# More spin matmuls in the first chunk, fillers and masks moved in units 5 and 6, and the last rows split 256 to 128

## The chip, the cores and the metric

The kernel runs on one core of a Trainium2 chip. The metric is device time in microseconds (us) of one execution; lower is better. Before the change, seven runs gave a median of 205.24 us, from 203.64 to 206.64. All times of single instructions come from one profiled execution.

The engines are called PE (matrix multiplication; its weight loads are listed as PEld), DVE (vector), ACT (activation and copies), POOL (the general engine GpSimd) and SP (which issues most transfers). Each works through its own queue in order, and they wait for one another through semaphores. PE writes to PSUM, from which DVE and ACT read.

## The reference

A recurrent attention layer with a decaying state, and after it a two-layer network. Batch 4, 8 heads, 768 steps, head width 48; the network goes from 384 to 2048 and back to 384, all in float32.

```python
def _attn_ref(r, k, v, w, u):
    for t in range(S):
        cur = np.einsum('bhd,bhe->bhde', u[None] * kt, vt)
        y[:, :, t] = np.einsum('bhd,bhde->bhe', rt, state + cur)
        state = w[None, :, :, None] * state + np.einsum('bhd,bhe->bhde', kt, vt)
    return y

def _moe_ref(x, w_in, w_out):
    h = x @ w_in
    g = h * (1.0 / (1.0 + np.exp(-h)))
    return g @ w_out
```

The output of the first, with the heads side by side (3072 x 384), is the input x of the second.

## The kernel before

The steps of time are cut into 6 chunks of 128, and a unit is one chunk of one batch: 24 units, numbered chunk by chunk, so that units 0 to 3 are the first chunk, 4 to 7 the second (B is 4 in the code). Inside a chunk the recurrence is written as a masked product, and the state is carried from chunk to chunk. The tiles run on a schedule written by hand: the order of the calls in the program is the order in each engine's queue.

For one unit the steps are these.

- `load` (lines 64 to 73): SP loads r, k and v, 192 KB each, into one of six sets of buffers.
- `nat_v`, `nat_ku`, `nat_rk`, `nat_kc` (172 to 192): ACT makes v in 16 bits; POOL makes ku = k times u, rku_f = r times ku, and kc, k scaled for the state.
- `p1` (214), or its two halves `p1t` (232) and `p1d` (249): PE transposes r and k into PSUM (tiles tr and tk, later xs), and DVE multiplies them by powers of the decay (tile rk).
- `bonus_sum` (194) and `bonus_vu` (200): DVE sums rku_f to rku, one number for each head, and POOL makes vu = v times rku. For unit 0, ACT makes vu (`bonus_act`, 207).
- `p2` (261): PE makes the score matrices ae and ao of the even and odd heads, and DVE masks them (tile am). With `nxt` given it also holds the transposes of the next unit, and their products unless `late` is set.
- `p3y` (283) and `p3e` (297): PE makes y from the masked scores and v, and from the second chunk on from the state; DVE adds vu and writes y in 16 bits (y16).
- `sums` (302) and `state` (312): PE makes the unit's share of the state (sps), DVE adds it to the state, and POOL decays it (sdec).
- `p4` (334): PE transposes y16 (yT), and ACT copies that into xT, the input of the network.

The network's work is a list of fillers. `l1` (348) makes 128 of the 2048 middle columns of one chunk: three matmuls on PE (tile hps) with w_in, and the activation on ACT (tile gT). `l2` (361) makes a quarter of the sum for 128 output rows (tile ops), four matmuls with w_out, and after the last quarter DVE copies the rows and SP stores them. `fill(n)` (397) takes fillers from the list up to a weight of n; a whole `l1` or an `l2` quarter weighs 1, an `l1` of two batches 0.5 (three matmuls of 256 columns). What a `fill` could not take is carried to the next one, up to a weight of 1.

The last 128 rows of output are made by `l2_last` (374), in two halves of 192 columns, each with 16 matmuls, a copy on DVE and a store.

w_in comes in four slices (`win_part`, 412) and w_out in two halves (`wout_part`, 416), issued by POOL in line with its other work: the first half of w_out at line 524, the second at line 530, after the `nat_kc` of unit 5.

`spin` (118) issues matmuls of 128 x 128 by 512 zeros, whose result nobody reads. Without a tile given it takes one from the five PSUM slots with the tag "t", which the transposes, scores, y, sps and yT share. Spins stand at the start (lines 137 and 139), before the transposes of unit 1 and before the scores of unit 1.

The order around the changed places is: `p2(1)`, rku and vu of unit 1, `p3e(0)`, `p3y(1)`, `p3e(1)`, `p4(0)`, `p1(2)`, the loads of the next chunk, `p4(1)`, and then the first fillers (lines 445 to 464). In the second chunk: `p2` of unit 5, fillers, `p3y`, `p3e`, `p1d` of unit 6, sums, fillers, `p4` of unit 5, fillers, a new list of fillers (542 to 554). From unit 6 on a loop (566 to 596) runs over the units.

Of the kernel before, what the change touches and what calls it, by code (L numbers as in the profile page):

```python
# [8 lines left out]
FP = mybir.dt.float32  # L9
# [6 lines left out]
def kernel(  # L16
# [11 lines left out]
    nc = tc.nc  # L28

    B, H, S, D = r.shape  # L30
    C = 128
    NCH = S // C
    HD = H * D
# [6 lines left out]
    NU = B * NCH  # L40
# [5 lines left out]
    wrk = ctx.enter_context(tc.tile_pool(name="wrk", bufs=2))  # L46
# [12 lines left out]
    wout = big.tile([128, NFT, HD], F16)  # L59

    def unit(i):
        return divmod(i, B)
# [29 lines left out]
    for t in (rin, kin):  # L92
# [7 lines left out]
        out=maskM, in_=maskM, compare_op=ALU.is_ge, fill=0.0,  # L100
# [17 lines left out]
    def spin(n, t=None):  # L118

        if t is None:  # L120
            t = ps.tile([128, 512], FP, name="spin", tag="t", bufs=5)
        else:
            t = t.rearrange("s p t -> s (p t)")
        for _ in range(n):
            nc.tensor.matmul(t, junk[:, 0:128], junk, start=True, stop=True)  # L125

    def to_cols(row, copy):
        t = ps.tile([128, 512], FP, name="cols", tag="t", bufs=5)
        nc.tensor.transpose(t[0:PR, 0:NP], row.rearrange("p j d -> p (j d)")[:, 0:PR],
                            ident[0:NP, 0:NP])  # L130
        if copy is None:
            return t[0:PR, 0:NP]
        c = cst.tile([PR, NP], FP, name="cols_sb")
        copy(out=c, in_=t[0:PR, 0:NP])
        return c

    spin(5)
    wT = to_cols(wrow, None)
    spin(5)
    u_bc = cst.tile([128, H, D], FP)  # L140
    lamC = cst.tile([128, H, D], FP)

# [12 lines left out]
    while n < C:  # L155
        nc.vector.tensor_tensor(
            out=pi[:, :, 1 + n:1 + 2 * n], in0=pi[:, :, 1:1 + n],
# [31 lines left out]
    def nat_kc(i):  # L189
        n = i % NIN  # L190
        nc.gpsimd.tensor_tensor(out=kc[i % NKC][:, :, 0:D], in0=kin[n][:, :, 0:D],  # L191
                                in1=lamC, op=ALU.mult)

    def bonus_sum(i):
        L = live[i]
        L["rku"] = wrk.tile([128, H], FP, name="rku", bufs=3)
        nc.vector.tensor_reduce(out=L["rku"], in_=L["rku_f"], axis=mybir.AxisListType.X,  # L197
                                op=ALU.add)
# [33 lines left out]
    def p1t(i):  # L232

        n = i % NIN
        L = live.setdefault(i, {})
        xs = [ps.tile([128, 2, NP, 64], FP, name="xs", tag="t", bufs=5) for _ in range(2)]
        for a, src in enumerate((rin, kin)):
            flat = src[n].rearrange("p h d -> p (h d)")
            for p in range(NP):
                for g in range(2):  # L240
                    t = slice(64 * g, 64 * g + 64)
                    nc.tensor.transpose(xs[g][0:PR, a, p, :],  # L242
                                        flat[t, 128 * p:128 * p + PR], ident[t, t])
        rk = wrk.tile([PR, 2, NP, C], FP, name="rk")
        L["rT"] = rk[:, 0]
        L["kT"] = rk[:, 1]
        L["xs"] = xs, rk

    def p1d(i):
        L = live[i]  # L250
        xs, rk = L["xs"]
        for g in range(2):
            nc.vector.tensor_tensor(out=rk[:, :, :, 64 * g:64 * g + 64], in0=xs[g][0:PR],  # L253
                                    in1=lam(g), op=ALU.mult)

    def r16(i):
        L = live[i]
        L["rT16"] = wrk.tile([PR, NP, C], F16, name="rT16")
        nc.scalar.copy(out=L["rT16"], in_=L["rT"])

    def p2(i, spins=0, nxt=None, late=False):
        L = live[i]
        ae = ps.tile([128, NP, C], FP, name="ae", tag="t", bufs=5)
        ao = ps.tile([128, NP, C], FP, name="ao", tag="t", bufs=5)
        spin(spins, ae)
        for p in range(NP):
            nc.tensor.matmul(ae[:, p, :], L["kT"][0:D, p, :], L["rT"][0:D, p, :],  # L267
                             start=True, stop=True)
            nc.tensor.matmul(ao[:, p, :], L["kT"][64:PR, p, :], L["rT"][64:PR, p, :],  # L269
                             start=True, stop=True)  # L270
        if nxt is not None:
            p1t(nxt)
        L["am"] = []
        for a in (ae, ao):
            am = wrk.tile([128, NP, C], F16, name="am", bufs=4)
            nc.vector.tensor_tensor(out=am, in0=a,  # L276
                                    in1=maskM.unsqueeze(1).broadcast_to([128, NP, C]),
                                    op=ALU.mult)
            L["am"].append(am)
        if nxt is not None and not late:  # L280
            p1d(nxt)

    def p3y(i):
        sc, b = unit(i)
        L = live[i]
        v16 = L["v16"]
        L["y"] = y = ps.tile([128, H, D], FP, name="y", tag="t", bufs=5)
        for p in range(NP):
            if sc:
                nc.tensor.matmul(y[:, 2 * p:2 * p + 2, :], L["rT16"][:, p, :],  # L290
                                 st16[b][:, p, :], start=True, stop=False)
            for j in range(2):
                nc.tensor.matmul(y[:, 2 * p + j, :], L["am"][j][:, p, :],  # L293
                                 v16[:, 2 * p + j, :], start=not sc,
                                 stop=(not sc or j == 1))

    def p3e(i):
        L = live[i]
        L["y16"] = wrk.tile([128, H, D], F16, name="y16")
        nc.vector.tensor_tensor(out=L["y16"], in0=L["y"], in1=L["vu"], op=ALU.add)  # L300
# [33 lines left out]
    def p4(i):  # L334
        sc, b = unit(i)
        L = live[i]
        if sc not in xts:
            xts[sc] = wrk.tile([128, NQ, B, C], F16, name="xT", bufs=3)
        yT = ps.tile([128, NQ, C], F16, name="yT", tag="t", bufs=5)
        yf = L["y16"].rearrange("p h d -> p (h d)")  # L340
        for q in range(NQ):
            nc.tensor.transpose(yT[:, q, :], yf[:, 128 * q:128 * q + 128], ident16)  # L342
        nc.scalar.copy(out=xts[sc][:, :, b, :], in_=yT)  # L343


    gts = {}
# [27 lines left out]
    def l2_last(sc, b):  # L374

        tt = b * S + sc * C
        for n0 in (0, HD // 2):
            ops = ps.tile([128, HD], FP, name="ops", tag="moe", bufs=3)
            for ft in range(NFT):
                nc.tensor.matmul(ops[:, 0:HD // 2], gts[sc][:, ft, b * C:(b + 1) * C],  # L380
                                 wout[:, ft, n0:n0 + HD // 2],
                                 start=(ft == 0), stop=(ft == NFT - 1))
            osb = wrk.tile([128, HD // 2], FP, name="osh")
            nc.vector.tensor_copy(out=osb, in_=ops[:, 0:HD // 2])
            nc.sync.dma_start(out=out[tt:tt + C, n0:n0 + HD // 2], in_=osb)

    def l1s(sc, b0=0, b1=B):
        return [((b1 - b0) / B, lambda ft=ft: l1(sc, ft, b0, b1)) for ft in range(NFT)]

    def l2s(sc, b0=0, b1=B):  # L390
        return [(1.0, lambda b=b, part=part: l2(sc, b, part))
                for b in range(b0, b1) for part in range(4)]
# [4 lines left out]
    def fill(n):  # L397
        owed[0] = min(owed[0] + n, n + 1.0)
        while fillers and owed[0] > 0.01:
            w_, f = fillers.pop(0)  # L400
            owed[0] -= w_
            f()
# [44 lines left out]
    bonus_vu(1)  # L447
    p3e(0)
    nat_kc(0)
    p3y(1)  # L450
    p3e(1)
    p4(0)
    p1(2)
    nat_ku(2)
# [5 lines left out]
    load(B + 1)  # L460
    p4(1)
    nc.scalar.copy(out=st[2], in_=zero)
    fillers.extend(l1s(0, 0, 2))
    fill(.5)
    nat_v(2)
# [31 lines left out]
    def front(i):  # L497
        nat_v(i)
        nat_ku(i)
        nat_rk(i)  # L500
        nat_kc(i)
# [38 lines left out]
        load(NIN + i)  # L540
    fill(.5)
    p2(b_, nxt=b_ + 1, late=True)
    fill(1)
    p3y(b_)
    p3e(b_)
    p1d(b_ + 1)
# [3 lines left out]
    load(NIN + 5)  # L550
    fill(.5)
    p4(b_)
    fill(1.5)
    fillers.extend(l1s(1, 0, 2) + l2s(0))
    sums(b_)
    state(b_)
# [8 lines left out]
    half_state(1)  # L565
    for i in range(B + 2, NU):
        sc, b = unit(i)
        bonus_sum(i)
        bonus_vu(i)
        p2(i, nxt=i + 1 if i + 1 < NU else None)  # L570
        fill(2)
        if i + 1 < NU:
            front(i + 1)
        if i >= NIN:
            load(i + NIN)
        fill(1)
        p3y(i)
        p3e(i)
        if sc < NCH - 1:
            sums(i)  # L580
            state(i)
        fill(2)
        p4(i)
        if i + 1 < NU:
            r16(i + 1)
        if i == B + 2:
            half_state(3)
        fill(1)
        if sc == 1:
            half_state(b)  # L590
        fill(2)
        if b == B - 1:
            if sc == 1:
                fillers.extend(l1s(1, 2, 4) + l2s(1))
            else:
                fillers.extend(l1s(sc) + l2s(sc))
# [32 lines left out]
```

## Time and profile before

| what | value |
|---|---|
| median of 7 runs | 205.24 us (203.64 to 206.64) |
| profiled execution: its own time | 204.11 us |
| profiled execution: span | 202.4 us |
| mean granted clock of PE | 0.992 |
| busy: PE, DVE, POOL, ACT | 192.5, 115.2, 115.0, 97.8 us |
| PE on ops (L366), hps (L354), scores (L267, in the chain) | 65.5 us, 70.3 us, 11% of the span |
| PE waiting for masks before y (L293) | 2.5 us |
| loads of r, k, v, issue to landing (median) | 3.5 to 3.8 us |
| w_out halves, issue to landing | 9.7 and 11.6 us |

The time of the execution is longer than the span by 1.7 us, what lies around the profiled program. A row of the page's table of groups reads: line, engine, operation, output from input, how many, then busy us and mean ns of one, then the idle time ahead of them and what ended it. The row of forty slices gives tenths of busy time; PEclk in it is the granted clock of PE in tenths. In the rows by stretches, each engine has its busy time and, in brackets, the number of its instructions. The chain of waits goes back from the last instruction, at each step to what released it; its rows give the start, the length, the engine, the tile and the line.

### The profile page before, as it was taken

The numbers are of one execution on the slowest core, as the hardware profiler recorded it, in microseconds if no ns is written. First come the engines' busy times: TensorE is split into PE (matmuls) and PEld (weight loads), VectorE is DVE, ScalarE is ACT, GpSimd is POOL, SyncE is SP. The second block draws the span as 40 slices with busy tenths as digits, with TensorE's granted clock in tenths as the row PEclk, the third lists the DMA queues.
The fourth block names the chain that finished last, engine by engine and source line by source line (L and its number), as shares of the span: only waits on it lengthen the run. The fifth ranks groups of instructions, "written<-read, shape, count | busy, mean of one in ns | idle before, by whom it ended". The sixth has DMA issues, their size and how long they took to land.

```text
span 202.4 us, 5004 instructions
## 1 busy us (share of the span) xinstructions
PE 192.5 (95%) x1967; PEld 130.7 (65%) x1967; DVE 115.2 (57%) x233; ACT 97.8 (48%) x225; POOL 115.0 (57%) x145
## 2 busy tenths in 40 slices
PE   7868999998999999999999999999999999999993
PEld 2647878786667777675666765666765666744563
DVE  6785658858559548595546865546864635510121
ACT  2564677797430680218772029772029661069300
POOL 3579967979954854957774757571738370100000
PEclk9996999999999999999999999999999999999999
DMA  4999999999999920759631639201120001110022
GB/s 85 201 191 154 175 223 181 180 186 200 175 226 219 225 49 28 169 125 219 129 63 56 144 95 190 45 0 42 39 79 3 0 3 40 70 50 0 0 78 78
DMA packets 82207, 22.34 MB, mean 110 GB/s; under 512 B 75400, under 2 KB 82184, under 8 KB 82184
## 3 DMA queue, kind: packets, MB, share of 16 engines
q1 hardware_dynamic: 78504, 18.88, 43.5%
q0 software_dynamic: 3680, 3.15, 10.4%
q8 instruction: 15, 0.25, 0.5%
q14 instruction: 8, 0.07, 0.1%
HBM read 20.45 MB, written 4.72 MB: 124 GB/s over the span
## 4 chain that ended last, share of the span: by engine, by line
PE 87%; DVE 6%; issue 2%; ACT 2%; POOL 1%; DVEq 0%; POOLq 0%
PE ops L366 30%; PE hps L354 27%; PE ae L267 11%; PE xs L242 4%; DVE am L276 3%; PE y L293 3%; PE yT L342 2%; PE spin L125 2%; PE y L290 2%; PE sps L309 1%; PE ops L380 1%; DVE y L300 1%; PE tk L223 1%; PE tr L223 1%; ACT xT L343 1%
## 5 line engine op out<-in xcount | busy, mean ns | idle before, releaser
L357 ACT ACTIVATE gT<-hps 128x256 f16<-128x256 f32 (+1 forms) x128 | 59.6, 493 | 25.6 <-PE hps L354 23.8
L354 PE MATMUL hps<-xT,win 128*128 128x256 f16 (+1 forms) x384 | 70.3, 327 | 1.0 <-ACT xT L343 0.6
L366 PE MATMUL ops<-wout,gT 128*128 128x384 f16 x368 | 65.5, 326 | 0.0
L354 PEld LDWEIGHTS <-win 128*128 128x128 f16 x384 | 35.2, 98 | 22.6 <-issue 1.6
L366 PEld LDWEIGHTS <-gT 128*128 128x128 f16 x368 | 34.2, 98 | 21.1
L343 ACT COPY xT<-yT 128x384 f16<-128x384 f16 x24 | 11.4, 476 | 58.8 <-PE yT L342 58.8
L276 DVE TENSOR_TENSOR am<-ae,maskM 128x512 f16<-128x512 f32 x24 | 16.6, 691 | 37.1 <-PE ao L269 36.9
L203 POOL TENSOR_TENSOR vu<-vin,rku 128x384 f32<-128x384 f32 x23 | 19.1, 829 | 21.1 <-DVE rku L197 21.0
L370 DVE COPY osb<-ops 128x384 f32<-128x384 f32 x23 | 12.8, 555 | 29.2 <-PE ops L366 29.0
L267 PEld LDWEIGHTS ae<-rk 48*128 48x128 f32 x192 | 23.2, 187 | 7.8 <-issue 5.7
L267 PE MATMUL ae<-rk 48*128 48x128 f32 x192 | 27.8, 285 | 0.4 <-DVE rk L230 0.4
L269 PE MATMUL ao<-rk 48*128 48x128 f32 x192 | 27.8, 285 | 0.0
L253 DVE TENSOR_TENSOR rk<-xs,pif 112x512 f32<-112x512 f32 x40 | 25.5, 680 | 1.7 <-PE xs L242 1.7
L186 POOL TENSOR_TENSOR rku_f<-rin,ku 128x384 f32<-128x384 f32 x24 | 24.1, 1005 | 1.9
L180 POOL TENSOR_TENSOR ku<-kin,u_bc 128x384 f32<-128x384 f32 x24 | 24.1, 1002 | 1.4 <-DMA kin<-in_k_dram 1.4
L191 POOL TENSOR_TENSOR kc<-kin,lamC 128x384 f16<-128x384 f32 x24 | 24.0, 1003 | 0.0
L269 PEld LDWEIGHTS ao<-rk 48*128 48x128 f32 x192 | 23.2, 187 | 0.0
L323 POOL CAST stb<-st 112x384 f16<-112x384 f32 x12 | 6.0, 502 | 25.8 <-DVE st L318 25.8
L300 DVE TENSOR_TENSOR y<-y,vu 128x384 f16<-128x384 f32 x24 | 13.3, 553 | 7.8 <-PE y L293 7.2
L276 DVE TENSOR_TENSOR am<-ao,maskM 128x512 f16<-128x512 f32 x24 | 16.3, 680 | 0.0
L197 DVE TENSOR_REDUCE rku<-rku_f 128x8 f32<-128x384 f32 x24 | 13.2, 549 | 3.8 <-POOL rku_f L186 3.4
L293 PE MATMUL y<-v,am 128*128 128x48 f16 x192 | 12.5, 185 | 2.8 <-DVE am L276 2.5
(74 smaller groups left out, 189.9 us busy)
## 6 DMA issues: line engine op xcount, KB each, us to landing
rin<-in_r_dram SPq DMA_DIRECT2D x24, 192.0 KB, 3.5
kin<-in_k_dram SPq DMA_DIRECT2D x24, 192.0 KB, 3.7
vin<-in_v_dram SPq DMA_DIRECT2D x24, 192.0 KB, 3.8
out_dram<-osb SPq DMA_DIRECT2D x23, 192.0 KB, 2.0
win<-in_moe_w_in_dram POOLq DMA_DIRECT2D x4, 384.0 KB, 5.7
wout<-in_moe_w_out_dram POOLq DMA_DIRECT2D x2, 768.0 KB, 10.6
out_dram<-osh SPq DMA_DIRECT2D x2, 96.0 KB, 1.6
wrow<-in_w_dram SPq DMA_DIRECT2D x1, 1.5 KB
```

Of the source, the lines that this page charges most:

```text
L180: nc.gpsimd.tensor_tensor(out=L["ku"], in0=kin[i % NIN][:, :, 0:D], in1=u_bc, op=ALU.mult)
L186: nc.gpsimd.tensor_tensor(out=L["rku_f"], in0=rin[i % NIN][:, :, 0:D], in1=L["ku"], op=ALU.mult)
L191: nc.gpsimd.tensor_tensor(out=kc[i % NKC][:, :, 0:D], in0=kin[n][:, :, 0:D], in1=lamC, op=ALU.mult)
L203: nc.gpsimd.tensor_tensor(out=L["vu"], in0=vin[i % NIN], in1=L["rku"].unsqueeze(2).broadcast_to([128, H, D]), op=ALU.mult)
L253: nc.vector.tensor_tensor(out=rk[:, :, :, 64 * g:64 * g + 64], in0=xs[g][0:PR], in1=lam(g), op=ALU.mult)
L267: nc.tensor.matmul(ae[:, p, :], L["kT"][0:D, p, :], L["rT"][0:D, p, :], start=True, stop=True)
L269: nc.tensor.matmul(ao[:, p, :], L["kT"][64:PR, p, :], L["rT"][64:PR, p, :], start=True, stop=True)
L276: nc.vector.tensor_tensor(out=am, in0=a, in1=maskM.unsqueeze(1).broadcast_to([128, NP, C]), op=ALU.mult)
L293: nc.tensor.matmul(y[:, 2 * p + j, :], L["am"][j][:, p, :], v16[:, 2 * p + j, :], start=not sc, stop=(not sc or j == 1))
L354: nc.tensor.matmul(hps, win[:, q, ft * 128:(ft + 1) * 128], xts[sc][:, q, b0:b1, :].rearrange("p b t -> p (b t)"), start=(q == 0), stop=(q ...
L357: nc.scalar.activation(out=gts[sc][:, ft, b0 * C:b1 * C], in_=hps, func=AF.Silu)
L366: nc.tensor.matmul(ops, gts[sc][:, ft, b * C:(b + 1) * C], wout[:, ft, :], start=(ft == 0), stop=(ft == NFT - 1))
```

## The change

It has four parts.

1. Spins: one fewer ahead of the first transposes (4 for 5), three new ones before `p3y(1)`, two before `p4(0)`, and two before the first fillers. The new ones take tiles of their own in the "t" slots.
2. Fillers: `fill(1)` before `p3y` of unit 5 becomes `fill(1.5)`, and `fill(1.5)` after its `p4` becomes `fill(1)`.
3. In the loop, for unit 6 only, `p2` goes ahead of `bonus_sum` and `bonus_vu`. On DVE the masks of unit 6 and the products of unit 7 now stand before rku of unit 6; PE's and POOL's orders are the same.
4. `l2_last` splits its 384 columns 256 and 128 instead of 192 and 192.

```diff
-    spin(5)
+    spin(4)
     u_bc = cst.tile([128, H, D], FP)
...
-        for n0 in (0, HD // 2):
+        for n0, n1 in ((0, 256), (256, HD)):
             ops = ps.tile([128, HD], FP, name="ops", tag="moe", bufs=3)
             for ft in range(NFT):
-                nc.tensor.matmul(ops[:, 0:HD // 2], gts[sc][:, ft, b * C:(b + 1) * C],
-                                 wout[:, ft, n0:n0 + HD // 2],
+                nc.tensor.matmul(ops[:, n0:n1], gts[sc][:, ft, b * C:(b + 1) * C],
+                                 wout[:, ft, n0:n1],
                                  start=(ft == 0), stop=(ft == NFT - 1))
-            osb = wrk.tile([128, HD // 2], FP, name="osh")
-            nc.vector.tensor_copy(out=osb, in_=ops[:, 0:HD // 2])
-            nc.sync.dma_start(out=out[tt:tt + C, n0:n0 + HD // 2], in_=osb)
+            osb = wrk.tile([128, HD], FP, name="osh")
+            nc.vector.tensor_copy(out=osb[:, n0:n1], in_=ops[:, n0:n1])
+            nc.sync.dma_start(out=out[tt:tt + C, n0:n1], in_=osb[:, n0:n1])
...
     p3e(0)
     nat_kc(0)
+    spin(3)
     p3y(1)
     p3e(1)
+    spin(2)
     p4(0)
     p1(2)
...
     p4(1)
     nc.scalar.copy(out=st[2], in_=zero)
+    spin(2)
     fillers.extend(l1s(0, 0, 2))
     fill(.5)
...
     p2(b_, nxt=b_ + 1, late=True)
-    fill(1)
+    fill(1.5)
     p3y(b_)
...
     p4(b_)
-    fill(1.5)
+    fill(1)
     fillers.extend(l1s(1, 0, 2) + l2s(0))
...
     for i in range(B + 2, NU):
         sc, b = unit(i)
+        if i == B + 2:
+            p2(i, nxt=i + 1)
         bonus_sum(i)
         bonus_vu(i)
-        p2(i, nxt=i + 1 if i + 1 < NU else None)
+        if i > B + 2:
+            p2(i, nxt=i + 1 if i + 1 < NU else None)
         fill(2)
```

## The prediction, made before the changed kernel had run

> **What bounds the kernel now.** I read the page first: the row of busy times and the row of forty slices.
>
> ```profile
> span 202.4 us, 5004 instructions
> ...
> PE 192.5 (95%) x1967; PEld 130.7 (65%) x1967; DVE 115.2 (57%) x233; ACT 97.8 (48%) x225; POOL 115.0 (57%) x145
> ...
> PE   7868999998999999999999999999999999999993
> ...
> PEclk9996999999999999999999999999999999999999
> ```
>
> PE is the bound, and full from about 50 us to the end. So what can be won is what PE loses ahead of 50 us, and the tail after its last matmul. Two things stand out there: thin slices up to 17 us, and one slice with the clock at 6 tenths. Busy time of PE by stretches of 3.41 us, laid so that one of them is the slow one (columns: stretch, length, PE busy, granted clock, DMA share, GB/s):
>
> ```profile
> 8.50:11.92 3.42, 3.26 (x39) 1.00 0.94 160
> 11.92:15.33 3.41, 1.66 (x28) 1.00 1.22 212
> 15.33:18.74 3.41, 2.84 (x17) 0.51 1.14 209
> ...
> 46.05:49.46 3.41, 2.76 (x36) 1.00 1.27 186
> ```
>
> PE was busy 49% of 11.92 to 15.33, and the next 3.41 us ran at half clock. A stretch with 81% (46.05) was followed by no drop, and 83% inside the slow stretch (2.84 of 3.41) was enough to raise the clock again. So the line lies between 49% and 81%. Third, the chain of waits over the slow place and over the last place where PE stands still:
>
> ```profile
> 12.89 1.27 DVE am L276 x2
> ...
> 14.62 0.47 DVE y L300
> ...
> 15.14 0.34 PE yT L342 x3
> 15.48 0.79 PE tr L223 x4
> 16.27 0.85 PE tk L223 x4
> 17.13 0.33 PE yT L342 x3
> ...
> 18.01 0.80 PE hps L354 x3
> ```
>
> ```profile
> 44.88 1.01 POOL rku_f L186
> ...
> 46.51 1.30 DVE am L276 x2
> ...
> 47.85 0.20 PE y L293
> ...
> 49.82 0.17 PE yT L342 x3
> ...
> 50.31 1.95 PE ops L366 x12
> ```
>
> In the first, PE waits for the masks and for y of unit 0, and then everything has double length. In the second, the mask of unit 6 stands behind a sum (rku) that waits for GpSimd.
>
> **The change, part by part** (times on the profiled execution, 204.11 us around a span of 202.4; the median of the seven runs is 205.24, 1.13 above it, so I carry differences over).
>
> *Spins in units 1 and 2.* At full clock a 512-column spin costs 0.216 us (the two at 11.26 take 0.43). PE's timeline shows idle times of 0.78 us before the first y of unit 1 (12.84 to 13.62), 0.57 before yT of unit 0 and 0.57 before the first hps. Three spins are 0.65, two are 0.43: each lot fits in its gap with 0.13 or more to spare, so they cost nothing while the clock is full. Their PSUM slots are free: in the instruction order, the first lot waits only for ACT's copy of lamC (11.30 to 11.78), the others for earlier PE work, and y of unit 1 no longer has that wait. PE's busy time in 11.92 to 15.33 rises from 1.66 to about 1.66 + 0.65 + 0.43 = 2.74, 80% (drains differ a little). That is beside the stretches that kept or raised the clock, so I take the clock to stay up.
>
> What that gives: tr 0.79 against 0.44 (the same four at 5.66), tk 0.85 against 0.44, yT 0.33 against 0.17, hps 0.80 against about 0.33 to 0.45: some 1.3 us less PE work before ae of unit 2. But another wait comes next on DVE's timeline:
>
> ```profile
> 18.56 0.55 DVE L197 TENSOR_REDUCE rku<-rku_f 128x8 f32<-128x384 f32 x1 [0.71 <-POOL rku_f L186]
> 19.96 0.69 DVE L276 TENSOR_TENSOR am<-ae,maskM 128x512 f16<-128x512 f32 x1 [0.84 <-PE ao L269]
> ```
>
> rku of unit 2 stands before its masks on DVE and waits for POOL, which is busy without a hole from 14.71 (vu, kc, ku, rku_f) and is not helped by PE. So the masks can start at 18.56 + 0.48 = 19.04 and not before: gain 0.92 of the 1.3. vu of unit 2 (20.10 to 20.94) then just precedes its use (20.98 instead of 21.76). Further on PE is full again, ft 8 of hps comes at 24.1, when the third slice of w_in has landed (POOL's queue is empty at 25.3 and that slice is the last but one), and xs of unit 4 comes at 27.9, after kin landed at 27.05. I carry 0.92; bounds 0 (clock drops anyway, or was no loss) and 1.3.
>
> [...]
>
> *One spin fewer at the start.* A spin there is 0.38 to 0.46, so tr and tk of unit 0 can come some 0.2 us earlier. The first product rk (6.61) then waits for the power chain on DVE (4.08 + 2.39 = 6.47). Bounds 0 and 0.1 gain; I take 0.
>
> *Fillers before y of unit 5.* Three hps matmuls (0.33) fill a hole of 0.27 at 38.84 to 39.11, but the list has only so many: after yT of unit 5 there are then none, and PE waits for xT there (ACT, to 41.18) 0.33 longer. DVE is unbroken through that stretch (am to 39.05, y 39.70) and sets both ends. Bounds -0.27 and +0.33; I take 0.
>
> *Masks of unit 6 before its rku.* ae ends at 44.3 in the time of before, so the masks can run 44.4 to 45.6 instead of 46.51 to 47.8, and y of unit 6 starts at 46.80, when the eighteen hps are done, without the waits of 0.25 and 0.40. sps and 12 hps follow, to 48.73. What is late next: rku, now behind masks and p1d of unit 7 (45.6 to 46.85), ends at 47.35; POOL takes vu at 47.60 as before (kc and sdec stand ahead), until 48.43; y16 to 49.0; so yT at 49.05 instead of 49.82. Gain 0.77; bounds 0 and 1.09 (49.82 - 48.73, if vu were no wait).
>
> *The second half of w_out.* It is issued by POOL at 39.34, took 11.6 us to land (the longest of its two; its queue shows the last packets between 50.5 and 51), so 50.94. Its first use is the ninth matmul of ops: 50.31 + 8 x 0.163 = 51.61. Slack today 0.67. With PE 1.69 earlier, that use is at 49.92. POOL's issue follows rku_f of unit 5 and comes about 0.9 earlier too, so landing is between 50.04 and 50.94, and the wait 0.1 to 1.0. I take 0.4, nearer the first, since the issue does move, but the DMA engines are full there (share 1.27) and the other loads take part of it back.
>
> *The last rows.* PE: 32 x 0.083 = 2.65 now; then 16 x 0.11 (hps of 256 columns, three in 0.33) + 16 x 0.057 (yT of 128 columns, three in 0.17) = 2.67: equal. The last copy has 128 columns: 0.557 for 384 and 0.358 for 192 give 1.04 ns a column, so 0.29 instead of 0.36. The last transfer is 64 KB instead of 96. The first issue (0.33) is over before the second is due.
>
> ```profile
> 196.51 2.65 PE ops L380 x32
> ...
> 199.19 0.36 DVE osh L384
> ```
>
> Gain 0.10; bounds: 0.17 gain, and 0.66 loss if a weight load per matmul (98 ns, the row of L366) set the pace of the narrow half (16 x 0.098 - 0.91). But today's 0.083 is already under the 98 ns of its loads, and yT's three in 0.17 load weights as well, hence the near end. [...]
>
> **Sum:** -0.92 + 0 + 0 - 0.77 + 0.4 - 0.10 = -1.39, so 202.72 for the profiled execution, 203.85 for the median, say 203.9.
>
> **Rivals** (profiled execution, median).
> 1. *The weights set the end.* w_out lands at 50.94 as now. Then only 0.67 and the tail's 0.10 come through: 203.34, 204.47. For it: 0.67 slack and a full DMA. Against: POOL issues it earlier.
> 2. *The clock falls anyway.* The line is higher than 80%, or a spin counts for less than its time. Then the two spins before hps take 0.86 against a hole of 0.57: +0.29 - 0.77 - 0.10 = -0.58: 203.53, 204.66. Against: the spins at the start go from 0.46 each (five in 2.31) to 0.38 (five in 1.90), later ones take 0.216: spins alone brought the rate up.
> 3. *Slower: w_out lands later than now.* Whatever PE wins before it is void; beyond 51.7 the kernel is slower than before. The two halves already differ by 1.9 us (9.7 and 11.6). At 52.5: +0.89 - 0.10 = +0.79: 204.90, 206.03. Against: nothing is added to the DMA's work, and its issue is earlier.
> 4. *All comes through:* no wait for w_out or for vu: -0.92 - 1.09 - 0.17 - 0.1 = -2.28: 201.83, 202.96.
>
> **How the numbers follow.** Forecast 0.45 (own range 203.0 to 204.7), rival 1 0.20, rival 2 0.10, rival 3 0.10, rival 4 0.15. The seven runs spread over 3 us, so I take 0.6 us around each median. 202.2 to 205.7 holds some eight in ten: rival 4's lower half and rival 3's upper part are out. A measurement of this kernel tells about 1% (2.05 us, that is 203.19) from no change: faster takes rival 4 mostly (0.12) and the lower part of the forecast (0.19), 0.31; slower (over 207.3) is the far end of rival 3, 0.06; the rest, 0.63, lies within.
>
> **What would show it.** Right: granted clock 1.00 in 15 to 19 us; masks of unit 2 at about 19.0, directly behind rku; no PE wait before y of unit 6, and a short one before its yT; ops' ninth matmul waiting 0.1 to 1 us for w_out; the last copy 0.29. Wrong: a slow stretch still there or moved, masks of unit 2 before rku_f is done, w_out landed before 49.9, or the last 16 matmuls over 1.2 us.

## The result, and the profile after

The changed kernel takes 202.70 us in the median of 25 runs (202.46 to 203.68); the kernel before, with all its runs by then, 204.03 (203.30 to 207.04, 62 runs); the medians are 1.33 apart. The ratio is 0.9924, with a 95% interval of 0.9905 to 0.9942: 1.55 us faster on 204.03, where 1.39 was forecast. The ratios leave out the few runs of a kernel that lie over 1.5% above its fastest. The median itself was forecast at 203.9, 1.2 higher than it came, because the first seven runs of before had a median of 205.24. The profiled execution took 202.87, 1.24 less than the one of before; the terms of the sum are held against that difference.

The page of the changed kernel (span, busy times, PE and granted clock in forty slices):

```profile
span 201.2 us, 5015 instructions
...
PE 192.7 (96%) x1973; PEld 129.8 (65%) x1973; DVE 115.1 (57%) x233; ACT 98.1 (49%) x225; POOL 115.1 (57%) x145
...
PE   7889999899999999999999999999999999999993
...
PEclk9999999999999999999999999999999999999999
```

The slice at 6 tenths is gone. The stretches around it, on the changed kernel (stretch, length, PE busy, granted clock, DMA share, GB/s):

```profile
11.86:15.28 3.42, 2.85 (x32) 1.00 1.22 212
15.28:18.69 3.41, 3.27 (x36) 1.00 1.21 217
```

83% where 49% was, and the clock stays. DVE's timeline has the masks of unit 2 where the prediction put them, directly behind rku, with POOL as the new limit (19.04 instead of 19.96):

```profile
18.57 0.55 DVE L197 TENSOR_REDUCE rku<-rku_f 128x8 f32<-128x384 f32 x1 [1.26 <-POOL rku_f L186]
19.04 0.68 DVE L276 TENSOR_TENSOR am<-ae,maskM 128x512 f16<-128x512 f32 x1
```

Unit 6 and the first use of w_out, on PE's timeline of the changed kernel:

```profile
48.17 0.34 PE L342 MATMUL yT<-ident,y 128*128 128x128 f16 x3 [0.28 <-DVE y L300]
48.35 0.49 PE L354 MATMUL hps<-xT,win 128*128 128x256 f16 x3
48.68 1.46 PE L366 MATMUL ops<-wout,gT 128*128 128x384 f16 x8
50.35 0.81 PE L366 MATMUL ops<-wout,gT 128*128 128x384 f16 x4 [0.21 <-DMA wout<-in_moe_w_out_dram]
```

The waits before y of unit 6 are gone, a shorter one stands before its yT, and after eight matmuls of ops PE waits for the second half of w_out. The chain of waits of the changed kernel names the length of that transfer, and further on the tail:

```profile
38.42 11.89 DMA wout<-in_moe_w_out_dram
```

```profile
195.42 2.65 PE ops L380 x32
198.07 0.02 issue
198.09 0.29 DVE osh L384
```

### The profile page after: what moved, and what is told of

It is laid out like the page before. It is cut to its first block, busy times and chain, and to the rows that moved or that the text cites. A ratio compares the mean times of both kernels' runs of the same rounds, so it can differ in the third digit from the quotient of the medians.

```text
span 201.2 us, 5015 instructions
## 1 busy us (share of the span) xinstructions
PE 192.7 (96%) x1973; PEld 129.8 (65%) x1973; DVE 115.1 (57%) x233; ACT 98.1 (49%) x225; POOL 115.1 (57%) x145
## 4 chain that ended last, share of the span: by engine, by line
PE 81%; DMA 6%; POOL 5%; ACT 2%; issue 2%; DVE 2%; DVEq 0%; POOLq 0%
PE ops L366 30%; PE hps L354 26%; PE ae L267 10%; DMA wout<-in_moe_w_out_dram 6%; PE xs L242 4%; PE y L293 2%; PE spin L125 2%; PE yT L342 2%; PE y L290 2%; POOL rku_f L186 2%; POOL ku L180 1%; PE sps L309 1%; PE ops L380 1%; DVE am L276 1%; POOL kc L191 1%
## 5 line engine op out<-in xcount | busy, mean ns | idle before, releaser
L325 POOL TENSOR_TENSOR sdec<-st,pif 112x384 f32<-112x384 f32 x16 | 13.3, 836 | 2.5 <-DVE st L318 1.4
```

## The experiments

All times in us. Each kernel is the changed one with the edit named, unless it says otherwise. Most have 12 runs; the kernel before, unaltered, and the one with the other order of the second layer have 8, the one with vu of unit 6 earlier has 6.

| kernel | median | single times |
|---|---|---|
| before | 204.03 | 203.30 to 207.04 |
| changed | 202.70 | 202.46 to 203.68 |
| changed, once more | 202.68 | 202.50 to 203.65 |
| without the seven spins | 203.15 | 202.51 to 204.94 |
| first lot of spins alone | 202.82 | 202.46 to 204.51 |
| rku of unit 6 first again | 203.20 | 203.03 to 204.16 |
| tail and fillers back | 202.90 | 202.63 to 204.40 |
| w_out issued earlier | 203.78 | 203.39 to 205.53 |
| later loads held back | 202.62 | 202.47 to 206.04 |
| before, masks first | 203.43 | 202.86 to 206.07 |
| before, unaltered | 205.30 | 203.22 to 207.09 |
| other order of the second layer | 202.49 | 202.45 to 202.78 |
| that, and vu of unit 6 earlier | 202.04 | 202.03 to 202.34 |
| that, without the seven spins | 202.31 | 202.04 to 205.50 |

For every run the record also lists the granted clock, averaged over the run. One stretch of 3.41 us at half clock takes about 0.008 from that average (0.5 x 3.41 / 202.4). The 113 runs of the kernel before that were taken beside the experiments fall into four groups by it:

| granted clock | slow stretches | runs | times |
|---|---|---|---|
| 0.998 to 1.000 | none | 46 | 203.17 to 204.07 |
| 0.992 | one | 11 | 204.12 to 204.21 |
| 0.981 to 0.983 | two | 43 | 205.22 to 206.03 |
| 0.975 | three | 13 | 206.60 to 207.16 |

The times of the groups don't overlap. Profiles of executions with 0.992, 0.983 and 0.975 show one, two and three slow stretches (the first profile of before, and two of the profiles below). The changed kernel has 0.997 or more in every run.

### What the spins do

**Without the seven spins.**

```diff
-    spin(3)
     p3y(1)
     p3e(1)
-    spin(2)
     p4(0)
...
-    spin(2)
     fillers.extend(l1s(0, 0, 2))
```

> The changed kernel without its seven new spins (the four at the start stay). My theory, the clock: PE is busy about half of the 3.41 us around 12 to 15 us, the granted clock falls to 0.5 for 3.41 us after it, masks of unit 2 start near 19.96 instead of 19.04, and the time rises by 0.92 less what the wait for w_out gives back (up to 0.5): 0.4 to 0.9 us above the changed kernel, and the single runs spread again over 2 to 3 us, in groups, as before the change. Rival, the spins are without effect because POOL sets the pace there: within 0.2 us of the changed kernel, with the same narrow spread.

Median 203.15, 0.45 above the changed kernel, single times up to 204.94. The fastest are equal (202.51 and 202.46), so the spins themselves cost nothing. But the profiled execution, one of the long ones (204.90), shows no fall of the clock at all; its excess over the changed kernel's profile is the wait for w_out, which lands at 52.35 instead of 50.31, by its chain of waits:

```profile
38.72 13.63 DMA wout<-in_moe_w_out_dram
52.35 0.04 issue
52.39 0.81 PE ops L366 x4
```

So the size is as expected, but not for the reason expected: only two of the twelve runs have a low clock (0.992 at 203.81, 0.982 at 204.94), and the other ten have a median of 203.0, still 0.3 above the changed kernel. What makes that 0.3 is open. This run doesn't show that the clock is the cause, and a second cause of long runs appears.

**The first lot alone.**

```diff
     spin(3)
     p3y(1)
     p3e(1)
-    spin(2)
     p4(0)
...
-    spin(2)
     fillers.extend(l1s(0, 0, 2))
```

> The changed kernel with only the three spins before y of unit 1, without the two lots of two. PE is then busy about 68% (1.66 + 0.65 of 3.41 us) where 49% made the clock fall and 80% kept it up. My theory says only that the line lies between: if under 68%, clock 1.00 and the time of the changed kernel within 0.1 us; if over it, the drop is there and 0.4 to 0.9 us slower. Rival, what counts is a single idle time rather than the share: the longest one is still 0.57, a little under the 0.78 of before the change, so no drop in any run.

Median 202.82, 11 of 12 runs within 203.2, and a granted clock of 1.000 in all twelve: the first three spins do nearly all of it. The stretches of its profile (204.51, again with a wait for w_out of 1.8), laid, as in all profiles here, on the steps of 3.41 us in which that execution's clock changes:

```profile
12.86:16.27 3.41, 2.41 (x24) 1.00 1.11 198
...
50.40:53.82 3.42, 1.83 (x24) 1.00 0.42 78
53.82:57.23 3.41, 3.41 (x49) 1.00 1.11 220
```

71% and even 54% were followed by full clock. The rival forecast no fall here either, but its reason doesn't hold: a single wait of 1.8, most of it in the stretch of 54%, was followed by full clock, where in the kernel before a longest wait of 0.78 was followed by half.

**The kernel before, once more, for its profile.**

> The kernel before the change, unaltered, for one more profile of it. Its single times lie in groups near 203.5, 205.25 and 206.65 us. Theory of the groups: each step of 1.7 us is one more stretch of 3.41 us at half clock in a place where PE has no slack; so an execution of the group at 205.25 shows a stretch of half clock after 50 us or one more than the profile at 204.11 has. Rival: the steps are late landings of w_out, and the clock is as in the first profile.

This execution took 205.28 and has two slow stretches, one behind the other, where the first profile of before (204.11) had one:

```profile
12.32:15.74 3.42, 1.66 (x25) 1.00 1.09 187
15.74:19.15 3.41, 2.84 (x18) 0.50 0.88 166
19.15:22.56 3.41, 3.41 (x28) 0.50 0.75 103
22.56:25.98 3.42, 3.42 (x45) 1.00 1.20 206
```

Again 49% before the fall. The 83% in the first slow stretch did not raise the clock this time, as the same share had in the first profile. So the difference between the two executions is one more slow stretch, directly behind the first and not after 50 us; the rival is out.

**The same question where nothing later covers it.** The fastest kernel below (the second layer's new order, and vu of unit 6 earlier), without the seven spins:

> The fastest kernel so far (second layer's first quarters in another order, vu of unit 6 earlier) without the seven new spins. There, nothing waits for w_out any more, so nothing later covers what a fall of the clock costs. Theory: in executions whose 3.41 us grid catches a share of PE under about 0.55 between 12 and 16 us, the clock falls for 3.41 us (0.9 us longer) or for 6.83 us (1.7 to 1.8 us longer); the others take 202.0. So two or three groups, near 202.0, 202.9 and 203.8, and the profile shows a slow stretch if its time is in an upper group. Rival, the spread of the single times came from w_out: narrow, 202.0 to 202.4, as with the spins.

Seven of twelve runs lie from 202.04 to 202.34, the others at 203.01, 204.08, 204.14, 205.45 and 205.50; with the spins all six were within 202.34. The seven have a granted clock of 1.000, the others 0.992 (203.01), 0.983 (204.08 and 204.14) and 0.975 (205.45 and 205.50): one, two and three slow stretches. The profiled execution (205.45) has three slow stretches:

```profile
11.12:14.53 3.41, 2.23 (x28) 1.00 1.22 211
14.53:17.94 3.41, 2.56 (x16) 0.50 1.19 201
17.94:21.36 3.42, 3.13 (x21) 0.50 0.60 89
21.36:24.77 3.41, 3.41 (x25) 0.50 1.16 183
24.77:28.18 3.41, 3.41 (x39) 1.00 1.20 237
```

Steps of about 1, 2 and 3.4 us, against 0.9 and 1.7 expected for one and two: a third stretch was not foreseen. The rival is out: the spread comes with the missing spins, and no wait for w_out is in this profile. With that the clock is shown as the cause of the groups, and the spins as what keeps it up.

### What unit 6 brings

**rku of unit 6 ahead of its masks again.**

```diff
-        if i == B + 2:
-            p2(i, nxt=i + 1)
         bonus_sum(i)
         bonus_vu(i)
-        if i > B + 2:
-            p2(i, nxt=i + 1 if i + 1 < NU else None)
+        p2(i, nxt=i + 1 if i + 1 < NU else None)
```

> The changed kernel with rku of unit 6 ahead of its masks again. My theory: PE waits 0.25 + 0.40 before y of unit 6 as before the change and comes 0.77 later to ops, but then no longer waits there for w_out (0.37 to 0.53 in the changed kernel), so only 0.2 to 0.4 us slower than the changed kernel. Rival, the masks bring all of their 0.77: 0.7 to 0.8 us slower.

Median 203.20: 0.50 slower, between the two theories. PE's timeline of this kernel has the two old waits before y and, in this execution (204.16), a landing of w_out as late as 51.62:

```profile
46.32 0.20 PE L293 MATMUL y<-v,am 128*128 128x48 f16 x1 [0.25 <-DVE am L276]
46.92 0.20 PE L293 MATMUL y<-v,am 128*128 128x48 f16 x1 [0.40 <-DVE am L276]
...
51.66 0.81 PE L366 MATMUL ops<-wout,gT 128*128 128x384 f16 x4 [0.98 <-DMA wout<-in_moe_w_out_dram]
```

yT starts at 48.72 there, w_out aside, and at 48.17 in the changed kernel: 0.55.

**The kernel before, with the masks of unit 6 first and nothing else.**

```diff
+        if i == B + 2:
+            p2(i, nxt=i + 1)
         bonus_sum(i)
         bonus_vu(i)
-        p2(i, nxt=i + 1 if i + 1 < NU else None)
+        if i > B + 2:
+            p2(i, nxt=i + 1 if i + 1 < NU else None)
```

> The kernel before the change, with only the masks of unit 6 put ahead of its rku. Theory: PE no longer waits 0.25 + 0.40 before y of unit 6, so the fastest runs are 0.3 to 0.8 us under the fastest before (203.2); the clock still falls near 15 us where the stretch of low PE share is caught, so runs still spread over 1.5 us or more. Rival, the groups of single times before the change (near 203.5, 205.25 and 206.65, 1.7 us apart, half of the 3.41 us of a slow stretch) come from the clock falling after the waits at 46 to 50 us: then the upper groups go with this edit alone.

Median 203.43; ratio to before 0.9978, interval 0.9940 to 1.0017, so not told from no change. But its seven runs without a fall of the clock have a median of 203.16, and the 15 such runs of before in the same lot 203.54; its other five (0.975 to 0.992) still reach 206.07. The masks move the floor by 0.4 and leave the spread, against the rival. In its profile (202.86) the clock stays up even after 54%:

```profile
13.22:16.63 3.41, 1.84 (x22) 1.00 0.97 160
16.63:20.05 3.42, 2.83 (x31) 1.00 0.83 154
```

### The wait for w_out

**The changed kernel once more.**

> The changed kernel once more, as the yardstick on the same chip for the others of this lot. 202.4 to 203.0 us in most runs. In the profiles of the experiments so far the second half of w_out took 11.9 to 13.6 us to land, its last few packets coming alone: if it takes over 12 us here, the profiled execution has a wait of 1 to 2 us at the ninth matmul of ops and is that much longer than the median.

Median 202.68. In the profiled execution (203.65) the second half of w_out took 12.67 to land instead of 11.89, both issued at 38.42, and PE waited 1.0. It landed 0.78 later, and the execution is 0.78 longer (203.65 against 202.87): PE has no slack behind that wait.

**w_out issued earlier.**

```diff
     nat_rk(a)
-    nat_kc(3)
+    wout_part(0)
...
     p3e(a)
-    wout_part(0)
+    nat_kc(3)
```

> The changed kernel with the issue of the first half of w_out and the kc of unit 3 changed for one another in POOL's queue (0.94 and 0.99 us each): the first half of w_out is issued near 29.2 instead of 34.9, kc of unit 3 comes where w_out was, five us before its use. My theory: the second half lands before 49.9, the wait of PE at the ninth matmul of ops goes, 0.4 to 0.5 us faster than the changed kernel. Rival, the DMA engines are full there and the loads of r, k, v pay: PE or POOL wait for a load instead, no gain or up to 0.5 us slower.

1.1 us slower: the rival. Both halves landed in 8.2, but the loads paid. The longest waits on PE in this profile, at 36 to 44 us, and the stretches around them:

```profile
PEld xs L242 <- DMA kin<-in_k_dram: 1.7, 1, 1.7
PE xs L242 <- DMA kin<-in_k_dram: 1.5, 1, 1.5
```

```profile
35.35:38.76 3.41, 1.87 (x35) 1.00 1.27 230
38.76:42.18 3.42, 3.42 (x35) 0.50 0.91 134
```

The wait for k of unit 6 left PE 55% busy, and the clock fell there: in this execution (205.53) the loss is double. The other eleven runs have a granted clock of 0.999 or more and a median of 203.77, so the 1.1 does not come from the clock; that it is this wait for k there too is likely, but only this execution was profiled.

**Later loads held back.**

```diff
-    for i in range(4):
+    for i in range(3):
         load(NIN + i)
...
-    load(NIN + 4)
-    load(NIN + 5)
...
         bonus_vu(i)
+        if i == B + 2:
+            nc.gpsimd.memset(rin[3][:, 0, 0:1], 0.0)
+            for n in range(3, 6):
+                load(NIN + n)
```

> The changed kernel with the loads of units 9, 10 and 11 held back behind one small memset of POOL after vu of unit 6 (near 47.5 us; the first of them is used near 59). Theory, the last packets of w_out share the DMA engines with those loads: w_out lands 1 to 3 us earlier, PE does not wait at ops, 0.4 to 0.5 us faster than the changed kernel in the middle, and the runs spread over less than 1 us. Rival, the tail of w_out's packets has another cause: landing as before, no gain; or the loads come too late for unit 9 and the time rises.

Median 202.62, no gain. w_out took 13.28 in the profiled execution (206.04), longer than in the changed kernel. But the test does not settle whether those loads delay its last packets: they were to be free near 47.5 (the expectation's estimate), four us before w_out landed at 51.87, and the DMA engines still moved 106 GB/s in 49.57 to 52.99, at a share of 0.54. What delays them stays open. The other eleven runs lie within 202.47 to 202.81, where those of the changed kernel once more lie within 202.50 to 203.32; no profile says why. This execution also shows what a long wait there costs when the clock follows it:

```profile
46.16:49.57 3.41, 3.14 (x37) 1.00 1.10 172
49.57:52.99 3.42, 1.65 (x14) 1.00 0.54 106
52.99:56.40 3.41, 3.41 (x36) 0.50 1.11 220
```

**Another order of the second layer's first quarters**, so that the second half of w_out is needed later:

```diff
-            opss[0] = ps.tile([128, HD], FP, name="ops", tag="moe", bufs=3)
-        ops = opss[0]
+            opss[b] = ps.tile([128, HD], FP, name="ops", tag="moe", bufs=3)
+        ops = opss[b]
...
-    fillers.extend(l1s(1, 0, 2) + l2s(0))
+    first = l2s(0)
+    first = first[0:2] + first[4:6] + first[2:4] + first[6:]
+    fillers.extend(l1s(1, 0, 2) + first)
```

> The changed kernel with the first quarters of the second layer in another order: the two quarters of the first 128 rows that need the first half of w_out, then the same two of the next 128 rows, and only then those that need the second half. Its first use moves behind eight more matmuls and the scores of unit 7, from 49.98 to about 52.8 us; nothing else moves. Theory, PE waits there for the last packets of w_out (0.4 us in one profile of the changed kernel, 1 to 2 us in others): the wait goes in all of them, 0 to 0.3 us faster in the middle, no run over 203.2. Rival, the wait only moves to another engine that is as late (vu of unit 6 on POOL, masks of unit 7): no gain.

Median 202.49, highest 202.78: 0.2 off the middle and 0.9 off the top. w_out took 11.9 in this profile too, as in the changed kernel, and no wait for it is left.

**On top of it, vu of unit 6 earlier.**

```diff
-    def state(i):
+    def state(i, dec=True):
...
-        if sc < NCH - 2:
+        if sc < NCH - 2 and dec:
+            decay(b)
+
+    def decay(b):
...
-    state(3)
+    state(3, dec=False)
...
-            p2(i, nxt=i + 1)
+            p2(i, nxt=i + 1, late=True)
         bonus_sum(i)
         bonus_vu(i)
+        if i == B + 2:
+            decay(3)
+            p1d(i + 1)
```

> As the kernel with the second layer's new order, and on top vu of unit 6 earlier: on POOL ahead of the decay of unit 3's state, on DVE rku of unit 6 between its masks and the products of unit 7. Theory: the wait of 0.28 us before yT of unit 6 goes, and as PE has no slack after it, 0.2 to 0.3 us faster than that kernel, near 202.2. Rival, PE has slack behind it (w_out, or rk of unit 7 now later on DVE): no gain.

Median 202.04, another 0.45; the fastest kernel of the study, 0.66 under the changed one, ratio to before 0.9903 (0.9872 to 0.9934). PE's timeline of it runs through unit 6 without a wait:

```profile
47.75 0.33 PE L346 MATMUL yT<-ident,y 128*128 128x128 f16 x3
47.92 0.49 PE L358 MATMUL hps<-xT,win 128*128 128x256 f16 x3
48.24 1.95 PE L370 MATMUL ops<-wout,gT 128*128 128x384 f16 x11
```

ops starts 0.44 earlier than in the changed kernel (48.24 against 48.68): the wait of 0.28 was worth more than its length. The timeline counts a wait from the end of the matmul before it (46.42 + 1.47 = 47.89 in the changed kernel); without a wait yT starts ahead of that end (47.75 here, where the hps before it run from 46.44 to 47.91).

### The small parts

```diff
-        for n0, n1 in ((0, 256), (256, HD)):
+        for n0 in (0, HD // 2):
...
     p2(b_, nxt=b_ + 1, late=True)
-    fill(1.5)
+    fill(1)
...
     p4(b_)
-    fill(1)
+    fill(1.5)
```

> The changed kernel with its two smallest parts undone: the last rows split 192 and 192 again, and the fillers of unit 5 back where they were. Theory: the last copy is 0.07 longer and the last store up to 0.1, the fillers change only which hole PE waits in (0.27 before y of unit 5 against 0.40 before the hps after yT, of which 0.07 stays): 0.07 to 0.2 us slower than the changed kernel in the middle, 202.8 to 202.9. Rival, the fillers carry part of the gain: 0.3 to 0.5 us slower.

Median 202.90, 0.2 slower; the fastest run 0.17. On PE's timeline of this kernel the hole before y is back, and the yT and its wait are as in the changed one (which has 39.38, with 0.22, and then a wait of 0.40 for xT before hps):

```profile
38.48 0.20 PE L293 MATMUL y<-v,am 128*128 128x48 f16 x1 [0.27 <-DVE am L276]
39.68 0.34 PE L342 MATMUL yT<-ident,y 128*128 128x128 f16 x3 [0.22 <-DVE y L300]
```

This execution runs 0.3 behind the one of the changed kernel already ahead of the edit (the first half of w_out is issued at 35.2 and 34.9). From yT to the hps behind xT it is 0.91 here (39.68 to 40.59) and 0.90 in the changed kernel (39.38 to 40.28): the fillers bring nothing. The last copy is 0.36 again; the 0.07 it takes longer and 0.1 for the last transfer are about what the fastest run lost.

## Why the prediction was right, step by step

- **The number.** Between the profiles it fits: 202.72 forecast, 202.87 measured. For the median it is in part luck. Forecast was 203.85, with an own range of 203.0 to 204.7; 202.70 lies below that, nearest to rival 4's 202.96, though rival 4's reason (no wait for w_out) was not what happened in the profile. And the median of before, 204.03, lies between two groups: 31 of the 62 runs are at 203.96 or less, the other 31 at 204.11 or more. From the runs without a fall (median 203.6) to the changed kernel it is 0.9, from those with one slow stretch 1.5, with two 2.6.
- **The clock.** Right: share 83% (80% forecast), no fall, masks of unit 2 at 19.04, POOL the next limit; y of unit 3 moved from 26.76 to 25.83, 0.93 against 0.92. Too narrow was the view of one profile: executions of before have from none to three slow stretches by their granted clock, and the one that was profiled belongs to the rarest group (11 of 113), so what the spins bring differs from execution to execution. That is why the ratio, over many runs, shows more (1.55) than the two profiles (1.24). The prediction gave no cause for the 3 us of spread; without slow stretches it is 1.2. That 83% raises the clock again, as the prediction read it, was so in its profile but not in the second one.
- **Waits, length and place of the falls.** The fall in the first profile of before came behind single waits of at most 0.78. The slow stretches lasted 3.41 there, 6.82 in the second profile of before and 10.24 in the fastest kernel without the spins, which is one, two and three times 3.41, and they began at 15.42, 15.74 and 14.53.
- **Masks of unit 6.** Right in kind, over-sized: 0.77 was forecast, 0.54 came. ops starts at 50.15 before and 48.68 after, 1.47 less, of which 0.93 is the clock. The step that failed is "yT at 49.05 instead of 49.82". The 49.82 is from the chain of waits, which lets a running matmul start only where the one before it ends; PE's timeline of before starts that yT at 49.66:

```profile
47.25 0.20 PE L293 MATMUL y<-v,am 128*128 128x48 f16 x1 [0.25 <-DVE am L276]
47.85 0.20 PE L293 MATMUL y<-v,am 128*128 128x48 f16 x1 [0.40 <-DVE am L276]
...
49.66 0.33 PE L342 MATMUL yT<-ident,y 128*128 128x128 f16 x3
49.82 0.49 PE L354 MATMUL hps<-xT,win 128*128 128x256 f16 x3
50.15 2.11 PE L366 MATMUL ops<-wout,gT 128*128 128x384 f16 x12
```

The new yT stands behind a wait, and there both views have the same start (yT of unit 5 before: 40.31 in both). Against 49.66 the same working gives 0.61.
- **w_out.** Right in kind: wait at the ninth matmul, 0.37 (50.35 against 48.68 + 8 x 0.163 = 49.98), with 0.4 forecast. Landing at 50.31, between the two ends (50.04, 50.94): the issue did move 0.92 (39.34 to 38.42), but the transfer took 11.89, 0.3 longer. That is not so in every execution: in the five profiles where PE waits longest for it (1.0 to 2.0 us, four of them the longest run of their lot) it took 12.7 to 13.6 and landed at 51.09 to 52.35, later than the 50.94 of before, which is rival 3's case; in the others it took 10.8 to 12.4, or 8.2 where it was issued earlier.
- **Tail.** Right: copy 0.29; the transfer lands in 1.5 instead of 1.6. The 32 matmuls take 2.65 as before: 1.76 for the 16 of 256 columns (195.42 to 197.18) and 0.89 for the 16 of the narrow half (to 198.07), some 0.056 each, where 0.057 was forecast and 0.098, the length of one weight load, was the far bound.
- **Fillers and the first spin.** Right, nothing: see above; rk of unit 0 at 6.60 for 6.61.

The sum as measured, with the last copy and the last transfer at its end: -0.93 - 0.54 + 0.37 - 0.07 - 0.1 = -1.27, and 1.24 was found between the profiles.

## What to carry to other kernels

Look at the clock row stretch by stretch, at the share of PE in each step of the clock (3.41 us here), and at the single times of many runs beside their granted clocks: groups of them can tell of a place that one profile happens to miss. Filling short waits with spins cost nothing here, where each lot fits in its hole (fastest runs 202.46 with the seven, 202.51 without), and it kept the clock up (granted 0.997 or more in every run of the changed kernel, 0.975 to 0.992 in 67 of the 113 of before). When a gain ends at a transfer that is late, need its data later before you issue it earlier: a new order of the consumers won 0.2 to 0.9, an earlier issue lost 1.1.

## What the runs showed of the hardware that was not expected

- The share of PE in a stretch, as the profile counts it, does not fix when the clock falls. It fell after 48, 49, 49, 55 and 65%, and stayed after 54, 54, 56 and 63 (48.53 to 51.95 and 14.40 to 17.81 without the spins) and 71%. What else counts is open; a share of 80% and more at full clock was not followed by a fall in any stretch looked at.
- The way up isn't fixed either: 83% in a slow stretch raised the clock once and not the next time, and one execution needed three stretches (75, 92 and 100%).
- In the profiles here the clock changes only in steps of 3.41 us, but these don't lie at the same times in every execution. The record of the clock has its first change at 5.18 us in the first profile of before and at 5.04 in that of the changed kernel; in the first, the later ones within the kernel are three and four steps behind it (15.42 and 18.83), and the other profiles have their falls at 14.53, 15.74, 38.76 and 52.99.
- w_out's last packets come late and thinly: 25 packets of its queue in 49.0 to 50.4 in the changed kernel, 15 in 50.0 to 52.4 without the spins. The slower of its two halves of 768 KB took 10.8 to 13.6 us to land (8.2 only where it was issued earlier).
